# Block-diagonal local probabilities and strip-wise pooled scores in a fused attention and channel-mix kernel

## The chip, the cores and the metric

The kernel runs as one launch on one core of one Trainium2 chip. The metric is the device time of that core in microseconds: 724.21 as the median of three runs, from 723.01 to 724.3.

The engines are named as in the profile: PE is TensorE (PEld its weight loads), DVE is VectorE, ACT is ScalarE, POOL is GpSimd, SP is SyncE, which here only starts DMA transfers.

## What is computed

The reference, cut to what matters. q, k and v are (8, 8, 576, 64): batch, heads, positions, head size. The width of the second half is 512, its hidden width 1024.

```python
# attention, for each batch and head
q_d, k_d, v_d = means over groups of 4 positions       # 144 positions
out_up    = repeat(softmax(q_d @ k_d.T / 8) @ v_d, 4)  # pooled attention
scores    = where(abs(i - j) < 4, q @ k.T / 8, -1e9)   # local band
out_local = softmax(scores) @ v
x = (out_up + out_local), heads side by side           # (8, 576, 512)

# channel mix
x_prev = x shifted by one position, 0 at the start of each batch
xk = mu_k * x + (1 - mu_k) * x_prev
xr = mu_r * x + (1 - mu_r) * x_prev
k  = maximum(xk @ w_k, 0)
out = sigmoid(xr @ w_r) * ((k * k) @ w_v)
```

The weights `w_k`, `w_v`, `w_r` come as float64 and are turned into float32 on the chip.

## The kernel before, in words

**Pairs and chunks.** Attention goes by pairs of heads: pair n = 4b + p holds heads 2p and 2p + 1 of batch b, 32 pairs in all. The two heads of a pair are the two halves of the 128 partitions (64 values each) and are called e = 0, 1 in the code. The channel mix goes by 18 chunks of 256 rows (`CT`); a chunk starts when the pairs of its batch are done. In full stage the attention of later batches runs in between the chunks.

**A pair's steps.** SP loads q and k (`load_raw`, L279, a tile called raw with four buffers), v summed up as four planes (`load_v4`) and v in windows of 32 keys (`load_windows`, `vw`: 24 query positions need 30 keys; one window for each of the 24 groups of 24 queries of a head, four of them, i = 0 to 3, above each other on 4 x 32 partitions, six such columns g a head). DVE transposes q and k by blocks of 32 (`turn_q` L320, `turn_k` L325; two alternating tiles, `qT` and `kz`, by the parity of the pair; from pair 8 on, `SPLIT`, `kz` has two planes, one for each head with zeros in the other half, so that one product serves both heads). POOL pools q, k and v (`pool_q`, `pool_k`, `pool_v`; `pool_v` is on DVE for the first `VDVE` pairs). ACT copies the last 16 pooled queries of each head into a part of `qd` that is zero elsewhere (`last_q`, L351, two instructions at L356).

**Scores and softmax.** Pooled scores need 144 x 144 for each head. They lie in one PSUM bank as three column groups: `down_pe` (L465, products L468) makes the first 128 queries of each head with four products on quarters of the array (64 values deep, 64 queries wide); `down_last` (L457, product L461) makes the last 16 queries of both heads in one product over the whole array, 128 x 128, in which all but 32 of the 128 columns are zero. Local scores (`score_pe`, L389) are 24 products of 32 queries by 64 columns on four strips of 32 columns of the array (L400; before pair 8 one product for each head). Both softmaxes are worked out on DVE, ACT and POOL (`score_top` to `score_norm`, `down_top` to `down_norm`). Local probabilities are transposed on DVE (`score_turn`, tile `at`); `spread` (L451) copies them with four ACT instructions into `bd`, whose zeros are set once: there, two groups of 32 partitions each (i = 0, 1 and i = 2, 3) share 48 columns block by block. Pooled probabilities are transposed on PE (`down_turn`) and copied by ACT (`down_copy`, tile `adT`).

**Output of a pair.** `av_pe` (L519) makes the upsampled part, four products of 144 columns (L527, 72 positions deep, two accumulated for each head, on the two column halves of the array), and the local part, 24 products of 48 columns (L533), each 64 deep on one quarter of the array: r = 0, 1 for the halves of the partitions, e for the head. ACT copies the pooled part out of PSUM (`av_up`, L555, instruction L558), and DVE adds both into x (`av_out`, L560, two instructions at L566).

**The run.** In full stage PE takes the products of one pair and the output of the pair before it together: `run_pe` (L545) issues `down_last(n)`, `av_pe(n - 1)`, `down_pe(n)`, `score_pe(n)`. The first four pairs have `score_both` (L540) and `av_pe` apart; pair 4 begins with `score_both` alone.

**The channel mix.** `diff` (L583, on POOL for the first two chunks) subtracts neighbouring positions; ACT and DVE scale and add (`mix_part`, `mix_add`, `mix_high`, `mix_low`). Every float32 product of the mix is made as three products of a rounded type (F32R) of high parts and remainders: `k_pe` (L624, products L629), `r_pe` (L660), `v_pe` (L678). Remainders of the hidden values are `k_low` (L644, instruction L648), on DVE, or on POOL for the first chunk and for f in `KLF`. The weights are turned, rounded and split in the first 130 us (`weight_scale` to `weight_low`, L206 to L274): 20 tiles, `WORDER`; their remainders are made on PE and ACT (tiles in `LOWPE`), on DVE (`LOWDVE`) or on POOL.

**What sets the order.** `Plan` is a list scheduler that runs while the program is written. Each step is added with its engine, an assumed time, a rank (a wished time), the tiles that it reads and writes, and the buffers that it takes. `order()` takes the engine that can start first, and on it the ready step with the lowest rank. The resulting order is fixed: each engine works through its queue in that order and waits where a step's inputs are not there. `PER` is the wished time of a chunk, `STEP0` and `STEP1` the wished distances of the first pairs.

## Time and profile before

| | before |
|---|---|
| median of three runs | 724.21 us (723.01 to 724.3) |
| the profiled execution | 722.32 us |
| its span in the trace | 720.5 us |
| mean granted clock of TensorE | 0.959 |
| busy share PE / PEld | 92% / 78% |
| busy share DVE / ACT / POOL | 67% / 65% / 42% |
| bytes moved by DMA | 62.19 MB, mean 86 GB/s |

The page of the profile cuts the span in 40 slices of 18 us and gives the busy share of each engine in tenths (9 is 90% or more). A group of instructions is shown with its line, engine, output and inputs, its shape, how often it occurs, its busy time, the mean of one in ns, and the idle time of its engine just before, with what ended most of it. A row of the timeline has the start in us, a duration, engine, line and operation; a float32 product counts as two PE instructions. Matmuls are pipelined, so the starts of PE rows say more than their durations.

### The profile page before, as it was taken

How to read it: one execution, taken by the hardware profiler on the slowest of the kernel's cores; microseconds unless marked ns; L12 is line 12 of the kernel's file. 1: busy time of each engine (PE TensorE's matmuls, PEld its weight loads, DVE VectorE, ACT ScalarE, POOL GpSimd, SP SyncE). 2: the span in 40 equal slices, each digit the busy share in tenths (PEclk: the TensorE clock that was granted, in tenths of full speed). 3: DMA queues.
4: the chain of work that ended last, by engine and by line, in shares of the span. 5: the costliest groups of instructions: out<-in, count | busy, mean ns of one | idle time of the engine just before them, and what ended most of it. 6: DMA issues, size and time to landing. Idle time of an engine off the chain costs nothing.

```text
span 720.5 us, 18491 instructions
## 1 busy us (share of the span) xinstructions
PE 660.0 (92%) x7352; PEld 564.5 (78%) x7352; DVE 482.8 (67%) x863; ACT 465.0 (65%) x1159; POOL 299.4 (42%) x362
## 2 busy tenths in 40 slices
PE   2676785798999999999999999999999999999997
PEld 1543674686888888888888888888888888988986
DVE  3785899857975797579655688667866874464111
ACT  2464684677776877586567667586768676644442
POOL 5414398864454544454333266353565341000000
PEclk9977886799999999999999999999999999999999
DMA  8999944664435343433234163342451100000000
GB/s 138 175 245 186 217 126 105 114 117 79 103 63 114 77 95 70 110 67 82 60 70 96 40 134 73 93 81 77 80 120 40 53 2 31 1 30 30 0 30 30
DMA packets 221849, 62.19 MB, mean 86 GB/s; under 512 B 205123, under 2 KB 214595, under 8 KB 221763
## 3 DMA queue, kind: packets, MB, share of 16 engines
q1 hardware_dynamic: 221762, 61.01, 39.8%
q8 instruction: 58, 0.95, 0.6%
q14 instruction: 29, 0.23, 0.1%
HBM read 51.55 MB, written 9.44 MB: 85 GB/s over the span
## 4 chain that ended last, share of the span: by engine, by line
PE 76%; DVE 7%; ACT 4%; POOL 4%; DMA 3%; SPq 3%; issue 1%; POOLq 0%; ACTq 0%; DVEq 0%
PE ps_g L629 25%; PE acc L678 23%; PE ps_r L660 14%; PE ps_v L533 3%; PE ps_a L400 3%; PE ps_v L527 3%; SPq L286 2%; PE ps_a L461 1%; DMA v<-in_v_dram 1%; DMA stgx<-in_moe_w_k_dram 1%; ACT ad L485 1%; PE ps_a L468 1%; ACT L485 1%; PE ps_t L508 1%; DVE mxd L475 1%
## 5 line engine op out<-in xcount | busy, mean ns | idle before, releaser
L629 PE MATMUL ps_g<-xkh,wkh 128*128 128x256 f32 x576 | 165.6, 287 | 1.8 <-ACT xkh L616 1.5
L629 PE MATMUL ps_g<-xkl,wkh 128*128 128x256 f32 x576 | 162.5, 282 | 0.7 <-DVE xkl L621 0.7
L629 PE MATMUL ps_g<-xkh,wkl 128*128 128x256 f32 x576 | 162.0, 281 | 0.0
L648 DVE TENSOR_TENSOR kl<-kk,kh 128x256 fp32r<-128x256 f32 x119 | 65.9, 554 | 95.8 <-ACT kh L641 90.0
L678 PE MATMUL acc<-wvh,kh 128*128 128x512 f32 x288 | 115.9, 402 | 2.9 <-ACT kh L641 2.9
L678 PE MATMUL acc<-wvl,kh 128*128 128x512 f32 x288 | 114.6, 398 | 2.7 <-POOL wvl L274 2.7
L678 PE MATMUL acc<-wvh,kl 128*128 128x512 f32 x288 | 114.9, 399 | 2.1 <-DVE kl L648 1.2
L629 PEld LDWEIGHTS ps_g<-xkh,wkh 128*128 128x128 f32 x576 | 109.9, 191 | 7.8 <-ACT xkh L616 1.8
L629 PEld LDWEIGHTS ps_g<-xkl,wkh 128*128 128x128 f32 x576 | 109.8, 191 | 4.6 <-DVE xkl L621 1.0
L629 PEld LDWEIGHTS ps_g<-xkh,wkl 128*128 128x128 f32 x576 | 111.1, 193 | 0.0
L634 ACT ACTIVATE kk<-ps_g 128x256 f32<-128x256 f32 x144 | 55.0, 383 | 81.6 <-PE ps_g L629 78.8
L428 POOL TENSOR_TENSOR sm<-sm,mx 128x384 f32<-128x384 f32 x28 | 28.2, 1007 | 98.5 <-DVE mx L423 81.6
L648 POOL TENSOR_TENSOR kl<-kk,kh 128x256 fp32r<-128x256 f32 x25 | 21.2, 850 | 110.8 <-PE acc L678 81.3
L678 PEld LDWEIGHTS acc<-wvh,kl 128*128 128x128 f32 x288 | 54.9, 191 | 15.6 <-DVE kl L648 1.8
L678 PEld LDWEIGHTS acc<-wvh,kh 128*128 128x128 f32 x288 | 54.8, 190 | 12.5 <-ACT kh L641 3.3
L678 PEld LDWEIGHTS acc<-wvl,kh 128*128 128x128 f32 x288 | 54.9, 190 | 11.7 <-POOL wvl L274 3.1
L641 ACT ACTIVATE kh<-kk 128x256 fp32r<-128x256 f32 x144 | 60.2, 418 | 4.6
L640 ACT ACTIVATE kk<-kk 128x256 f32<-128x256 f32 x144 | 60.2, 418 | 4.3
L455 ACT ACTIVATE bd<-at 32x288 f32<-32x288 f32 x128 | 56.3, 440 | 9.6 <-DVE at L448 7.8
L475 DVE TENSOR_REDUCE mxd<-ps_a 128x3 f32<-128x432 f32 x32 | 19.4, 606 | 61.9 <-PE ps_a L400 56.9
L660 PE MATMUL ps_r<-wrh,xrh 128*128 128x512 f32 x144 | 57.6, 400 | 0.9 <-DVE sig L682 0.9
L660 PE MATMUL ps_r<-wrh,xrl 128*128 128x512 f32 x144 | 57.0, 396 | 0.0
(107 smaller groups left out, 1413.4 us busy)
## 6 DMA issues: line engine op xcount, KB each, us to landing
vw<-in_v_dram SPq DMA_DIRECT2D x126, 96.0 KB
qraw<-in_q_dram SPq DMA_DIRECT2D x128, 72.0 KB
kraw<-in_k_dram SPq DMA_DIRECT2D x128, 72.0 KB
v<-in_v_dram SPq DMA_DIRECT2D x32, 288.0 KB
out_dram<-sig SPq DMA_DIRECT2D x36, 256.0 KB
stg<-in_moe_w_k_dram SPq DMA_DIRECT2D x6, 512.0 KB
stgx<-in_moe_w_v_dram SPq DMA_DIRECT2D x4, 512.0 KB
stg<-in_moe_w_v_dram SPq DMA_DIRECT2D x4, 512.0 KB
```

The costliest lines, as they stand in the source:

```text
L400: nc.tensor.matmul(ps[32 * i:32 * i + 32, o:o + 64], qT[:, QT * j:QT * j + 32], kz[:, :, QT * j:QT * j + 32], start=True, stop=True)
L428: nc.gpsimd.tensor_tensor(out=s3, in0=s3, in1=mx[:, :, None].broadcast_to([P, 12, 32]), op=ALU.subtract)
L455: nc.scalar.activation(dst, src, AF.Copy)
L475: nc.vector.tensor_reduce(out=mx, in_=down_part(d["ps"]), axis=AX.X, op=ALU.max)
L527: nc.tensor.matmul(pv[0][64 * e:64 * e + 64, 288:432], d["vd"][:, 2 * e + kt, :], d["adT"][:, kt, 144 * e:144 * e + 144], start=(kt == 0), ...
L629: nc.tensor.matmul(ps, w[:, p, P * f:P * f + P], y[:, p, :], start=(m == 0), stop=(m == len(mm) - 1))
L634: nc.scalar.activation(kk, kq[c, f], AF.Relu)
L640: nc.scalar.activation(kk, kk, AF.Square)
L641: nc.scalar.activation(kh, kk, AF.Copy)
L648: eng.tensor_tensor(out=kl, in0=kk, in1=kh.bitcast(F32), op=ALU.subtract)
L660: nc.tensor.matmul(ps, y[:, p, P * t:P * t + P], w[:, p, :], start=(m == 0), stop=(m == len(mm) - 1))
L678: nc.tensor.matmul(accs[c][t], x[:, P * t:P * t + P], w[:, f, :], start=(f == 0 and m == 0), stop=(f == NF - 1 and m == 2))
```

## The change

Seven edits, made together:

1. **The local part of the output.** `bd` becomes 96 columns wide instead of 48, and `spread` puts each of the four groups of 32 partitions into 24 columns of its own, so that the whole 128 partitions form one block-diagonal matrix. `av_pe` takes 12 products of 96 columns, 128 deep, on the two column halves of the array (e), instead of 24 of 48 columns on quarters. The positions then lie in order in PSUM, and `av_out` reads and writes them in one stretch for each half.
2. **The pooled scores.** Pooled k is written into two planes (`kds`, one for each head, zeros in the other half), as `kz` is. `down_pe` makes the first 128 queries of each head with eight products of 32 queries on four strips of 32 columns of the array, and the last 16 queries with four more on the same strips. The product over the whole array (`down_last`) is gone, and with it `last_q` on ACT: `qd` is 176 columns wide, and the columns behind 144 are zeros, which the last strip reads along with the last 16 queries.
3. **The run.** `run_pe` issues `av_pe(n - 1)`, `down_pe(n)`, `score_pe(n)`; nothing of pair n stands ahead of the output of n - 1 any more, and pooled scores stand ahead of the local ones in `score_both` too.
4. **Buffers.** Raw q and k have three buffers instead of four.
5. **The band mask** is loaded twice by DMA into its double tile, instead of once and copied on POOL.
6. **Who makes what.** `LOWPE` takes weight tiles 9 and 11 as well, `LOWDVE` 8, 10, 12 and 14 (before, POOL made these six); `VDVE` is 2 instead of 4, so `pool_v` of pairs 2 and 3 goes to POOL; `KLF` is empty, so the `k_low` of f = 3 go to DVE.
7. **The planner's numbers**: `PER` 31.5 instead of 33.5, `STEP0` 6.0 and `STEP1` 0.0 instead of 4.0 and 4.0, and assumed times of the changed steps.

The diff, cut to its core:

```diff
-LOWPE = tuple(range(8))
-VDVE = 4
+LOWPE = (0,1,2,3,4,5,6,7,9,11)
+VDVE = 2
-LOWDVE = ()
+LOWDVE = (8,10,12,14)
-KLPOOL, KLF = 1, (3,)
+KLPOOL, KLF = 1, ()
-PER = 33.5
-STEP0, STEP1, W0, WSTEP = 4.0, 4.0, -25.0, 2.0
+PER = 31.5
+STEP0, STEP1, W0, WSTEP = 6.0, 0.0, -25.0, 2.0
...
-    qds = [cp.tile([P, 272], F32, name=f"qd{i}") for i in range(2)]
-    bd = cp.tile([P, 12, 48], F32, name="bd")
+    qds = [cp.tile([P, 176], F32, name=f"qd{i}") for i in range(2)]
+    kds = [cp.tile([P, 2, 144], F32, name=f"kd{i}") for i in range(2)]
+    bd = cp.tile([P, 12, 96], F32, name="bd")
...
-        raw = wp.tile([P, 18, 32], F32, tag="raw", name=nm + "raw", bufs=4)
+        raw = wp.tile([P, 18, 32], F32, tag="raw", name=nm + "raw", bufs=3)
...
-    def last_q(n):
-
-        qd = qds[n % 2]
-        for e in range(2):
-            h = slice(64 * e, 64 * e + 64)
-            nc.scalar.activation(qd[h, 144 + 16 * e:160 + 16 * e], qd[h, 128:144], AF.Copy)
-
...
-        nc.gpsimd.tensor_tensor(out=kd, in0=tk[:, :, 0], in1=tk[:, :, 1], op=ALU.add)
-        d["kd"] = kd
+        for e in range(2):
+            h = slice(64 * e, 64 * e + 64)
+            nc.gpsimd.tensor_tensor(out=kd[h, e, :], in0=tk[h, :, 0], in1=tk[h, :, 1], op=ALU.add)
...
-            dst, src = bd[32 * i:32 * i + 32, :, QT * (i % 2):QT * (i % 2) + QT], d["at"][32 * i:32 * i + 32, :, 0:QT]
+            dst, src = bd[32 * i:32 * i + 32, :, QT * i:QT * i + QT], d["at"][32 * i:32 * i + 32, :, 0:QT]
...
-        nc.tensor.matmul(ps[:, D0 + DP:D0 + DP + 144], d["qd"][:, 144:272], d["kd"], start=True, stop=True)
...
     def down_pe(n):
...
+        for t in range(4):
+            for e in range(2):
+                o = D0 + 2 * DP * e
+                nc.tensor.matmul(ps[32 * t:32 * t + 32, o:o + 144], qd[:, 32 * t:32 * t + 32], kd[:, e, :],
+                                 start=True, stop=True)
         for e in range(2):
-            for h in range(2):
-                o = D0 + 2 * DP * e
-                nc.tensor.matmul(d["ps"][64 * h:64 * h + 64, o:o + 144],
-                                 d["qd"][64 * e:64 * e + 64, 64 * h:64 * h + 64], d["kd"][64 * e:64 * e + 64, :],
-                                 start=True, stop=True)
+            o = D0 + DP
+            nc.tensor.matmul(ps[32 * e:32 * e + 32, o:o + 144], qd[:, 128:160], kd[:, e, :], start=True, stop=True)
+            nc.tensor.matmul(ps[64 + 32 * e:96 + 32 * e, o:o + 144], qd[:, 144:176], kd[:, e, :], start=True, stop=True)
...
         for g in range(NG):
-            for r in range(2):
-                h = slice(64 * r, 64 * r + 64)
-                for e in range(2):
-                    nc.tensor.matmul(pv[r][64 * e:64 * e + 64, 48 * g:48 * g + 48],
-                                     d["vw"][h, 6 * e + g, :], bd[h, 2 * g + e, :], start=True, stop=True)
+            for e in range(2):
+                nc.tensor.matmul(pv[g // 3][64 * e:64 * e + 64, 96 * (g % 3):96 * (g % 3) + 96],
+                                 d["vw"][:, 6 * e + g, :], bd[:, 2 * g + e, :], start=True, stop=True)
...
     def run_pe(n):
-        down_last(n)
-        av_pe(n - 1)
-        down_pe(n)
-        score_pe(n)
+        av_pe(n - 1)
+        score_both(n)
```

How instructions move. The queue of PE in a run of full stage, between two groups of products of the mix, before the change: `kd` and `qd` are pooled k and q, `adT` and `bd` the probabilities, `vd` and `vw` the values.

```order
L461 MATMUL ps_a<-kd,qd_76 128x144
L527 MATMUL ps_v<-adT,vd 64x144 x4
L533 MATMUL ps_v<-bd,vw 64x48 x24
L468 MATMUL ps_a<-kd,qd_76 64x144 x4
L400 MATMUL ps_a<-kz_79,qT_82 32x64 x24
```

The same run after the change:

```order
L518 MATMUL ps_v<-adT,vd 64x144 x4
L522 MATMUL ps_v<-bd,vw 64x96 x12
L457 MATMUL ps_a<-kd_77,qd_75 32x144 x8
L461 MATMUL ps_a<-kd_77,qd_75 32x144
L462 MATMUL ps_a<-kd_77,qd_75 32x144
L461 MATMUL ps_a<-kd_77,qd_75 32x144
L462 MATMUL ps_a<-kd_77,qd_75 32x144
L393 MATMUL ps_a<-kz_80,qT_83 32x64 x24
```

The product over the whole array at the head is gone, the local part has half as many products of twice the columns, and the pooled scores are twelve products in a row.

The queue of ACT at the end of the first batch, before the change. The last `av_up` of the batch (L558, second row of that line) stands behind `last_q` of pair 4 (L356); L241, L259 and L269 turn weights.

```order
L558 ACTIVATE up<-ps_v 128x144
L269 ACTIVATE wkl<-ps_w 128x512
L259 ACTIVATE wkh<-w_612 128x512
L259 ACTIVATE wkh<-w_753 128x512
L241 ACTIVATE w_793<-stgx 128x512
L269 ACTIVATE wkl<-ps_w 128x512
L241 ACTIVATE w_838<-stgx 128x512
L356 ACTIVATE qd_75<-qd_75 64x16 x2
L558 ACTIVATE up<-ps_v 128x144
L259 ACTIVATE wvh<-w_793 128x512
```

The same place after the change, with `av_up` at L545:

```order
L545 ACTIVATE up<-ps_v 128x144
L448 ACTIVATE bd<-at 32x12x24 x4
L509 ACTIVATE adT<-ps_t 72x288 x2
L266 ACTIVATE wkl<-ps_w 128x512
L256 ACTIVATE wkh<-w_642 128x512
L238 ACTIVATE w_771<-stg 128x512
L545 ACTIVATE up<-ps_v 128x144
L256 ACTIVATE wkh<-w_692 128x512
L266 ACTIVATE wkl<-ps_w 128x512
```

Between the last two `av_up` of the batch, `last_q` is gone and fewer weight steps stand there.

The queue of POOL at the same place, before the change; L587 is `diff` of the first chunk, L373 and L374 are `pool_v`, L348 to L365 pool q and k of pair 4.

```order
L373 TENSOR_TENSOR v_657<-v_657 72x4x128
L374 TENSOR_TENSOR vd<-v_657 72x256
L348 TENSOR_TENSOR tq<-qT_81 128x288
L349 TENSOR_TENSOR qd_75<-tq 128x144
L364 TENSOR_TENSOR tk<-kz_78 128x288
L365 TENSOR_TENSOR kd<-tk 128x144
L373 TENSOR_TENSOR v_717<-v_717 72x4x128
L374 TENSOR_TENSOR vd<-v_717 72x256
L587 TENSOR_TENSOR dx<-xt 128x1024
L648 TENSOR_TENSOR kl<-kk,kh 128x256
```

The same place after the change, with `diff` at L573 and `pool_v` at L365 and L366:

```order
L365 TENSOR_TENSOR v_660<-v_660 72x4x128
L366 TENSOR_TENSOR vd<-v_660 72x256
L573 TENSOR_TENSOR dx<-xt 128x1024
L365 TENSOR_TENSOR v_714<-v_714 72x4x128
L366 TENSOR_TENSOR vd<-v_714 72x256
L634 TENSOR_TENSOR kl<-kk,kh 128x256
```

`diff` stands ahead of the second `pool_v` instead of behind it, and pooling of q and k of pair 4, ahead of `diff` before, comes behind these rows.

More of the change, by code (lines that the diff above doesn't have):

```diff
@@ L394, in score_pe @@
             for e in range(2):
-                nc.tensor.matmul(ps[:, S1 * e:S1 * e + 32 * NG], idn, mask, start=True, stop=False)
+                nc.tensor.matmul(ps[:, S1 * e:S1 * e + 32 * NG], idn, mask2[:, :, 0, :], start=True, stop=False)
         for j in range(4 * NG):
@@ L510, in down_turn @@
             nc.tensor.matmul(ps.rearrange("p (e c) -> p e c", e=2)[:, :, 128:144], ak[1],
-                             idn[:, 0:32].rearrange("p (e c) -> p e c", e=2), start=True, stop=True)
+                             idn[:, 0:64].rearrange("p (e c) -> p e c", e=2)[:, :, 0:16], start=True, stop=True)
     def down_copy(n):
@@ L529, in av_pe @@
         for g in range(NG):
-            for r in range(2):
-                h = slice(64 * r, 64 * r + 64)
-                for e in range(2):
-                    nc.tensor.matmul(pv[r][64 * e:64 * e + 64, 48 * g:48 * g + 48],
-                                     d["vw"][h, 6 * e + g, :], bd[h, 2 * g + e, :], start=True, stop=True)
+            for e in range(2):
+                nc.tensor.matmul(pv[g // 3][64 * e:64 * e + 64, 96 * (g % 3):96 * (g % 3) + 96],
+                                 d["vw"][:, 6 * e + g, :], bd[:, 2 * g + e, :], start=True, stop=True)
         d["pv"] = pv
@@ L540, in score_both, with run_pe @@
     def score_both(n):
-        down_last(n)
-        score_pe(n)
-        down_pe(n)
-    def run_pe(n):
-        down_last(n)
-        av_pe(n - 1)
+        st[n]["ps"] = pp.tile([P, 1024], F32, tag="att", name="ps_a", bufs=1)
         down_pe(n)
         score_pe(n)
+    def run_pe(n):
+        av_pe(n - 1)
+        score_both(n)
     def new_x(b):
@@ L686, in store_out @@
         nc.sync.dma_start(outf[r0:r0 + P, :], gates[c][t])
-    plan = Plan(dict(raw=4, v4=2, vw=3, kd=2, sm=2, ad=1, adT=1, at=1, up=2, vd=2, xt=2, f32tmp=2, xkh=2,
+    plan = Plan(dict(raw=3, v4=2, vw=3, sm=2, ad=1, adT=1, at=1, up=2, vd=2, xt=2, f32tmp=2, xkh=2,
                      xkl=2, xrh=1, xrl=1, kk=2, kh=4, kl=4, sig=3, g=2, acc0=1, acc1=1, c0=1, c1=1, att=1))
@@ L722, in pair_scores @@
             add("POOL", 1.2, R - 7, pool_q, n, r=[f"qT{i}"], w=[f"qd.{i}"])
-            add("ACT", 0.42, R - 6, last_q, n, w=[f"qd.{i}"])
-            add("POOL", 1.4 if n < SPLIT else 2.0, R - 6, pool_k, n, r=[f"kT{i}"], new=[(f"kd{n}", "kd")])
+            add("POOL", 1.9 if n < SPLIT else 2.4, R - 6, pool_k, n, r=[f"kT{i}"], w=[f"kd.{i}"])
             add(*(("DVE", 1.0) if n < VDVE else ("POOL", 2.15)), R1 - 8, pool_v, n, r=[f"v4{n}"], new=[(f"vd{n}", "vd")])
@@ L851, in begin_all @@
     def begin_all():
-        add("SP", 1.0, -110, load_consts, w=["mask", "idn"])
-        add("POOL", 2.2, -110, clear, w=["kT0", "kT1", "qT0", "qT1", "qd.0", "qd.1", "bd"])
+        add("SP", 1.5, -110, load_consts, w=["mask", "idn"])
+        add("POOL", 2.2, -110, clear, w=["kT0", "kT1", "qT0", "qT1", "qd.0", "qd.1", "kd.0", "kd.1", "bd"])
         add("SP", 1.0, W0, load_mus, w=["mu"])
@@ L857, in attention_moe @@
     add("ACT", 0.3, -60, turn_sign, r=["idn"], w=["nidn"])
-    add("POOL", 1.0, -60, double_mask, r=["mask"], w=["mask2"])
     for i in range(len(WORDER)):
@@ L879, in attention_moe @@
                 else:
-                    add("PE", 3.3 if n < SPLIT else 2.85, at_run[n], run_pe, n, **join(av_of(n - 1), s))
+                    add("PE", (3.0 if n < SPLIT else 2.6) - 0.15, at_run[n], run_pe, n, **join(av_of(n - 1), s))
                     pair_scores(n - 1, 2)
```

24 lines of the change are left out of this document (9 added, 15 removed).

## The prediction

> **What bounds the kernel now.** I read the page first (busy shares, slices, the chain that ended last), then the windows, then single stretches of the timeline. On the page:
>
> ```profile
> PE 660.0 (92%) x7352; PEld 564.5 (78%) x7352; DVE 482.8 (67%) x863; ACT 465.0 (65%) x1159; POOL 299.4 (42%) x362
> ...
> PE   2676785798999999999999999999999999999997
> ...
> PE 76%; DVE 7%; ACT 4%; POOL 4%; DMA 3%; SPq 3%; issue 1%; POOLq 0%; ACTq 0%; DVEq 0%
> ```
>
> TensorE carries three quarters of the chain, and its holes lie in the first eight of 40 slices. The windows put numbers to that; the columns are the busy times of PE, PEld, DVE, ACT and POOL, then clock, DMA share and GB/s:
>
> ```profile
> 60.00:80.00 20.00, 12.17 (x134) 8.06 (x135) 13.72 (x18) 13.48 (x28) 6.29 (x8) 0.67 1.00 187
> 80.00:100.00 20.00, 16.22 (x80) 13.34 (x79) 17.49 (x21) 13.39 (x34) 14.67 (x11) 0.81 0.72 189
> 100.00:120.00 20.00, 15.90 (x222) 12.39 (x220) 19.17 (x26) 13.89 (x36) 18.45 (x18) 0.83 0.54 131
> 120.00:135.00 15.00, 6.58 (x171) 5.27 (x171) 13.84 (x20) 7.94 (x19) 12.82 (x15) 0.56 0.49 88
> 135.00:180.00 45.00, 42.17 (x489) 35.69 (x490) 30.30 (x60) 33.60 (x85) 26.74 (x35) 0.99 0.53 103
> 180.00:600.00 420.00, 417.37 (x4807) 363.44 (x4806) 304.73 (x560) 297.44 (x750) 192.43 (x232) 1.00 0.35 77
> ```
>
> So there are two stages with different limits. From 135 on TensorE is idle for 2.8 us of 45 and 2.6 us of 420: there every microsecond that its instructions gain or lose is a microsecond of the end, and DVE, ACT and POOL have a quarter or more of their time free. Before 135 TensorE waits; DMA is full to 80, DVE and POOL are nearly full from 80 to 135. There only an earlier arrival of 134.9 counts, where the second chunk's first product (L629) starts and TensorE stays busy. The forecast is the sum of the two.
>
> **Part 1: the run of small products after 135.** A run (`run_pe`) in the full stage, block by block; the column behind the start is the modelled busy time, so I take starts:
>
> ```profile
> 324.14 0.41 PE L461 MATMUL ps_a<-kd,qd 128*128 128x144 f32 x2
> 324.48 0.71 PE L527 MATMUL ps_v<-adT,vd 72*64 72x144 f32 x8
> 325.12 0.91 PE L533 MATMUL ps_v<-bd,vw 64*64 64x48 f32 x48
> 325.86 0.44 PE L468 MATMUL ps_a<-kd,qd 64*64 64x144 f32 x8
> 326.23 0.88 PE L400 MATMUL ps_a<-kz,qT 128*32 128x64 f32 x48
> 327.04 0.39 PE L629 MATMUL ps_g<-xkh,wkh 128*128 128x256 f32 x1
> ```
>
> The blocks take 0.34, 0.64, 0.74, 0.37 and 0.81, together 2.90 us. A float32 product is two passes, so the count is double. How long a pass is, the last two rounds of L527 show (two narrow windows):
>
> ```profile
> 324.78 0.41 PE L527 MATMUL ps_v<-adT,vd 72*64 72x144 f32 x4
> ```
>
> ```profile
> 324.90 0.29 PE L527 MATMUL ps_v<-adT,vd 72*64 72x144 f32 x2
> ```
>
> A round (one pass on each column half at the same time) of 144 columns takes 0.12 us, 0.85 ns a column. L461 is two passes one behind the other, 0.24, in 0.34: a block that ends with another split of the array costs about 0.10 more. L468 is two rounds on four quarters, 0.24, in 0.37: 0.10 for its end and 0.03 for the first round after a switch.
>
> The new run, term by term: the switch from the big products to column halves, 0.10 (now paid behind L461); the upsampled part, unchanged, 0.64 less its closing switch, 0.54, as the local part now uses the same halves; the local part, 12 products = 24 passes of 96 columns on two halves = 12 rounds of 0.08, with its switch 1.08 (0.74 now); the pooled scores, 12 products = 24 passes on four strips = 6 rounds of 0.12 and 0.03, 0.75 (0.34 + 0.37 = 0.71 now); the local scores, 0.81 less the 0.02 to 0.03 of a first round, 0.79, as they already run on strips. Sum 3.26: **0.36 us more a run**. Four quarters at work become two halves, with twice the columns, and that costs more than the switch saved. From below: L533's rounds take 0.74/12 = 0.06 where 48 columns would need 0.04, so something besides columns limits them; were 96 columns to cost no more rounds than that, the local part would be 0.84 and the pooled scores 0.71, and the run 2.98, still 0.08 up. From above see the second rival. Pairs 7 to 31 have 25 runs after 135: 25 x 0.36 = 9.0, and the last local part by itself 0.2: **+9.2 us** (2 at the least).
>
> Hidden in this stage, by the free time of the window 180 to 600 (DVE 115 us, ACT 123, POOL 228):
>
> ```profile
> L356 ACT ACTIVATE qd<-qd 64x16 f32<-64x16 f32 x64 | 13.5, 211 | 24.7 <-POOL qd L349 24.2
> L365 POOL TENSOR_TENSOR kd<-tk 128x144 f32<-128x144 f32 x32 | 17.7, 555 | 2.5
> L648 DVE TENSOR_TENSOR kl<-kk,kh 128x256 fp32r<-128x256 f32 x119 | 65.9, 554 | 95.8 <-ACT kh L641 90.0
> ```
>
> ACT loses the 64 copies of `last_q` (13.5 us); POOL writes pooled k in two halves, at most 32 more additions of 0.56 (18 us); DVE takes the 17 `k_low` of f = 3 from POOL (9.4 us). `spread` writes as many elements, `av_out` as many. All nothing here, and a few tenths each if DVE's cover went. Three raw buffers: SP's queue waits for the transpose of the third load back; 25 runs in the 465 us from 135 to 600 are one in 18 us or so, and DMA is a third full, so nothing; otherwise a late `turn_k` would stop TensorE at the next run, in front of the pooled scores.
>
> **Part 2: the start.** Where the time to 134.9 is lost now: the last attention output of the first batch.
>
> ```profile
> 55.38 0.71 PE L527 MATMUL ps_v<-adT,vd 72*64 72x144 f32 x8
> 56.02 0.92 PE L533 MATMUL ps_v<-bd,vw 64*64 64x48 f32 x48
> ```
>
> ```profile
> 61.47 0.44 ACT L356 ACTIVATE qd<-qd 64x16 f32<-64x16 f32 x2 [4.41 <-POOL qd L349]
> 61.93 0.29 ACT L558 ACTIVATE up<-ps_v 128x144 f32<-128x144 f32 x1
> ```
>
> ```profile
> 62.26 0.82 DVE L566 TENSOR_TENSOR xt<-ps_v,up 128x288 f32<-128x288 f32 x2 [4.14 <-ACT up L558]
> ```
>
> ```profile
> 58.25 1.26 POOL L373 TENSOR_TENSOR v<-v 72x512 f32<-72x512 f32 x1 [11.28 <-DMA v<-in_v_dram]
> 59.59 0.72 POOL L374 TENSOR_TENSOR vd<-v 72x256 f32<-72x256 f32 x1
> ...
> 66.59 1.26 POOL L373 TENSOR_TENSOR v<-v 72x512 f32<-72x512 f32 x1 [3.90 <-DMA v<-in_v_dram]
> 67.93 0.72 POOL L374 TENSOR_TENSOR vd<-v 72x256 f32<-72x256 f32 x1
> 68.62 1.89 POOL L587 TENSOR_TENSOR dx<-xt 128x1024 f32<-128x1024 f32 x1
> ```
>
> The product is done at 56.9, but `av_up` stands in ACT's queue behind `last_q` of the next pair, which waits for POOL and that for a load; and on POOL `diff` stands behind a second `pool_v`, which waits for its load until 66.6. With `last_q` gone, x could be whole at 56.9 + 0.29 + 0.82 = 58.0. In the new POOL order `diff` stands behind one `pool_v` only, that of pair 4, done at 60.3. So `diff` starts at 60.3, not 68.6: **8.3 us earlier**, bound by the same load as now. The two chances that x is later than 60.3 (two `pool_v` moved from DVE to POOL, 2.0 us each, ahead of the norms of pairs 2 and 3; two more words to write per pooled k, 4 x 0.56) have 2.3 us of slack.
>
> How much of that reaches 134.9? From 80 on POOL and DVE hold it:
>
> ```profile
> 128.50 1.29 POOL L365 TENSOR_TENSOR kd<-tk 128x144 f32<-128x144 f32 x1
> ```
>
> ```profile
> 134.90 0.58 PE L629 MATMUL ps_g<-xkh,wkh 128*128 128x256 f32 x1
> ```
>
> ```profile
> L274 POOL TENSOR_TENSOR wvl<-w,wvh 128x512 fp32r<-128x512 f32 x4 | 6.9, 1722 | 1.2 <-PE ps_g L629 1.2
> L274 POOL TENSOR_TENSOR wkl<-w,wkh 128x512 fp32r<-128x512 f32 x4 | 6.6, 1642 | 4.0 <-ACT wkh L259 4.0
> L682 DVE TENSOR_TENSOR sig<-acc,sig 128x512 f32<-128x512 f32 x36 | 23.9, 682 | 5.0 <-PE acc L678 4.9
> ```
>
> POOL is rid of six weight remainders (four k, two v: 4 x 1.64 + 2 x 1.72 = 10.0 us), DVE gets four of them, by its nearest row of this width 0.68 each, 2.7 us, and TensorE two, in its idle time. DVE is the fuller engine (19.17 of 20), so its 2.7 count. But DVE's steps are longer beside POOL's:
>
> ```profile
> 108.53 1.64 DVE L255 SCALAR_TENSOR_TENSOR w<-stgx,w 128x512 int32<-128x512 int32 x1
> ```
>
> ```profile
> 115.12 0.69 DVE L255 SCALAR_TENSOR_TENSOR w<-stg,w 128x512 int32<-128x512 int32 x1
> ```
>
> The first ran while POOL was busy, the second in POOL's pause: up to 0.95 apiece, 5.7 for the six. I take a quarter, 1.4, since POOL has other work to put there. So the start gains 8.3 - 2.7 + 1.4 = **7.0 us**. From below 0 (if all of it is lost again by 134.9), from above about 13: 8.3 and half of POOL's 10.0.
>
> **Sum.** +9.2 - 7.0 = +2.2. The profiled execution took 722.32 us for a span of 720.5; the median of the runs is 724.21, 1.9 above it. So 724.5 for such an execution, and 726.4 as a median.
>
> **Rivals.**
>
> *POOL's relief decides (faster).* The last wait before 134.9 is for POOL (pooled k, 128.50 to 129.79, behind those eight remainders and more). If POOL and not DVE is what limits 100 to 135, the start gains 13 and not 7: 9.2 - 13 = -3.8, 720.4. For it: 18.45 of 20 on POOL. Against: DVE's 19.17. It decides from a gain of 9.2 on; the second chunk's first product would start before 125.7.
>
> *The strips go one after another (much slower).* The new loop issues both heads' products of a strip, four passes, before the next strip. If a strip holds one waiting pass beside the running one and the third stops the queue, each strip starts 0.24 behind the one before and the block ends after 1.44, not 0.75: 0.69 x 25 = 17 more, 743.6. For it: no row has four passes in a row on one part of the array with others behind. Against: L468's passes come in pairs on each quarter and still ran four at a time: 0.37; in strict order of program they would take 4 x 0.12 + 0.12 = 0.60. The Trainium skill, "TensorE: Matmul & The Clock Gate", Part 3 (packing small matmuls), says that matmuls start and end in program order without reordering; the trace of L468 does not agree. By that rule the block would take 2.04, the run 1.3 more, 32 in all, 758.7 us; after L468's row I give it 0.02 of the 0.21 below.
>
> *The start gives nothing.* With three raw buffers the k load of pair 5 waits for the transpose of pair 4's q, which in the new DVE order stands behind the first chunk's mixing; if pairs 5 and 6 then arrive as late as now or nearly, a start gain of 0 to 2 leaves +9.2 to +7.2: 732. For it: DMA is full until 80. Against: pair 5's run stands behind the first chunk's k products and most of its v products in both orders.
>
> **Chances and range.** Forecast 0.42, faster rival 0.27, strips 0.21, start 0.10. A measurement of this kernel tells 0.2%, 1.4 us, from no change. The forecast's own spread (about 3 us: the quarter taken of 5.7, the 0.08 to 0.36 of the run) gives 0.29 slower, 0.11 same, 0.02 faster; the faster rival 0.26 faster and 0.01 same; the strips 0.21 slower; the last 0.07 slower and 0.03 same. Together 0.28 faster, 0.15 same, 0.57 slower. The range goes from 717 (the faster rival with a start gain of 16, 8.3 and most of POOL's 10.0) to 745 (the strips at their price); the forecast's own is 722 to 731.
>
> **What would show it.** In the changed profile: the local part's 24 passes take about 1.0 us from their first start to that of the pooled scores, in a full run; the pooled scores 0.75 (1.4 or 2.0: the strips); the whole run 3.26. `diff` of the first chunk starts near 60.3, and the second chunk's first `ps_g` product near 128; after it TensorE is idle for no more than some 6 us to the end. I am wrong if the run is not longer than 2.98, if that product starts before 125.7 or after 132, or if a wait for q or k raw data shows in front of a run.

## The result, and the profile after

The changed kernel takes 732.52 us as the median of four runs (731.45 to 733.98), beside 723.61 (720.89 to 724.3) for the kernel before. The ratio is 1.0126, with an interval from 1.0107 to 1.0145: slower by 1.3%, or 9 us. The profiled execution after took 732.89 us with a span of 731.1; before it was 722.32 and 720.5, so between the two traces there are 10.6 us.

The forecast was 726.4 and the range 717 to 745: the sign and the range held, and the size did not; the forecast's own spread, 722 to 731, was missed from above. Of its two parts the run came out at its forecast price of 0.36 us within a few hundredths, and the start with the wrong sign. The boundary is the second chunk's first product, which before started at 134.90. These are the rows of the two traces that fix the parts; first the changed kernel's timeline of TensorE, a wait and that product:

```profile
134.06 1.23 PE L518 MATMUL ps_v<-adT,vd 72*64 72x144 f32 x8 [11.31 <-DVE xt L551]
...
139.70 0.39 PE L615 MATMUL ps_g<-xkh,wkh 128*128 128x256 f32 x1
```

So the start lost 4.8 us (139.70 against 134.90) where 7.0 were to be gained. From there to the end it is 731.1 - 139.70 = 591.4 us, against 720.5 - 134.90 = 585.6 before: 5.8 more, where 9.2 were forecast.

**The run.** A run in the full stage of the changed kernel, block by block (start, modelled busy time):

```profile
307.52 0.28 PE L615 MATMUL ps_g<-xkh,wkl 128*128 128x256 f32 x1
307.73 0.71 PE L518 MATMUL ps_v<-adT,vd 72*64 72x144 f32 x8
308.27 1.16 PE L522 MATMUL ps_v<-bd,vw 128*64 128x96 f32 x24
309.36 0.72 PE L457 MATMUL ps_a<-kd,qd 128*32 128x144 f32 x16
309.87 0.30 PE L461 MATMUL ps_a<-kd,qd 128*32 128x144 f32 x2
...
310.12 0.87 PE L393 MATMUL ps_a<-kz,qT 128*32 128x64 f32 x48
310.92 0.39 PE L615 MATMUL ps_g<-xkh,wkh 128*128 128x256 f32 x1
```

From start to start: upsampled part 0.54, local part 1.09, pooled scores 0.76, local scores 0.80. The last product of the mix ahead of it is followed after 0.21 instead of the usual 0.12, which is the switch of some 0.10. Together 3.29 us, against 2.90 before.

**Waits of TensorE after 135**, grouped by who releases them; before the change:

```profile
PE ps_t L508 <- POOL ad L496: 3.1, 4, 1.1
PE acc L678 <- DVE kl L648: 1.2, 1, 1.2
PE ps_r L660 <- DVE sig L682: 0.9, 2, 0.6
PE ps_g L629 <- ACT kk L634: 0.3, 1, 0.3
```

and after it:

```profile
PE ps_t L500 <- POOL ad L488: 1.1, 1, 1.1
PE ps_r L646 <- DVE sig L668: 0.7, 2, 0.5
```

5.5 us have become 1.8. That is 3.7 us which the forecast did not have, and it offset part of the run's price: 25 x 0.39 = 9.75, less 3.7, is 6.1, close to the 5.8 measured.

**The start.** In the changed kernel POOL's `diff` (L573), behind the `pool_v` of pair 4:

```profile
62.71 1.26 POOL L365 TENSOR_TENSOR v<-v 72x512 f32<-72x512 f32 x1 [11.96 <-DMA v<-in_v_dram]
64.05 0.72 POOL L366 TENSOR_TENSOR vd<-v 72x256 f32<-72x256 f32 x1
64.73 1.89 POOL L573 TENSOR_TENSOR dx<-xt 128x1024 f32<-128x1024 f32 x1
```

and what waits for it on DVE, the first `mix_add`, while the steps on weights stand behind it:

```profile
68.39 1.23 DVE L598 TENSOR_TENSOR xk<-xk,xt 128x1024 f32<-128x1024 f32 x1 [7.87 <-ACT xk L584]
69.53 1.77 DVE L247 SCALAR_TENSOR_TENSOR w<-stgx,w 128x512 int32<-128x512 int32 x1
```

`diff` starts at 64.7, where the forecast had 60.3 and the kernel before 68.6. DVE, the engine with the most work in this stage, stands still for 7.9 us. The whole account of DVE up to the second chunk's first product (window; busy time of PE, PEld, DVE, ACT, POOL; clock, DMA share, GB/s) is, before the change

```profile
0.00:134.90 134.90, 83.62 (x1311) 62.19 (x1311) 103.21 (x162) 75.90 (x193) 74.64 (x89) 0.79 0.83 166
```

and after it

```profile
0.00:139.70 139.70, 83.93 (x1270) 62.61 (x1271) 100.89 (x162) 73.64 (x179) 76.03 (x95) 0.80 0.80 159
```

DVE has 162 instructions in both. Its busy time went down from 103.2 to 100.9 us and its idle time up from 31.7 to 38.8. Busy and idle time add up to the window by definition, so the account says where the loss lies, idle time, and not yet why. Two entries of the list of idle times in these windows, by line, show the largest part of it (x count, busy time, mean ns, and the idle time just before); before the change

```profile
L323 DVE STREAM_TRANSPOSE qT<-qraw 128x576 f32<-128x576 f32 x8 | 6.1, 760 | 7.1 <-DMA qraw<-in_q_dram 7.1
L612 DVE TENSOR_TENSOR xk<-xk,xt 128x1024 f32<-128x1024 f32 x2 | 2.4, 1208 | 1.5 <-ACT xk L598 1.5
```

and after it

```profile
L320 DVE STREAM_TRANSPOSE qT<-qraw 128x576 f32<-128x576 f32 x8 | 6.1, 764 | 10.6 <-DMA qraw<-in_q_dram 10.6
L598 DVE TENSOR_TENSOR xk<-xk,xt 128x1024 f32<-128x1024 f32 x2 | 3.5, 1754 | 7.9 <-ACT xk L584 7.9
```

The hole in front of the mix grew by 6.4 us. Waits of DVE for the loads of q, k and v grew from 11.1 to 18.7 in all, and its waits for ACT's `av_up` shrank from 5.0 to 0.8.

### The profile page after: what moved, and what is told of

Its sections match the earlier page's. It is cut to its first block, busy times and chain, and to the rows that moved or that the text cites. A ratio compares the mean times of both kernels' runs of the same rounds, so it can differ in the third digit from the quotient of the medians.

```text
span 731.1 us, 17865 instructions
## 1 busy us (share of the span) xinstructions
PE 669.8 (92%) x7038; PEld 582.2 (80%) x7038; DVE 482.7 (66%) x880; ACT 452.3 (62%) x1097; POOL 298.1 (41%) x375
## 4 chain that ended last, share of the span: by engine, by line
PE 81%; DVE 6%; issue 4%; DMA 3%; ACT 2%; SPq 2%; POOL 2%; DVEq 0%; ACTq 0%; POOLq 0%
PE ps_g L615 27%; PE acc L664 24%; PE ps_r L646 14%; PE ps_v L522 4%; PE ps_a L457 3%; PE ps_v L518 3%; PE ps_a L393 2%; SPq L283 1%; DMA stgx<-in_moe_w_k_dram 1%; ACT ad L477 1%; DVE w L247 1%; PE ps_t L500 1%; PE ps_a L461 1%; DMA kraw<-in_k_dram 1%; PE ps_t L501 1%
## 5 line engine op out<-in xcount | busy, mean ns | idle before, releaser
L634 DVE TENSOR_TENSOR kl<-kk,kh 128x256 fp32r<-128x256 f32 x136 | 71.8, 530 | 103.9 <-ACT kh L627 103.2
L664 PE MATMUL acc<-wvh,kl 128*128 128x512 f32 x288 | 113.3, 393 | 2.8 <-POOL kl L634 2.7
L664 PE MATMUL acc<-wvl,kh 128*128 128x512 f32 x288 | 112.4, 390 | 1.1 <-POOL wvl L271 1.1
L615 PEld LDWEIGHTS ps_g<-xkh,wkl 128*128 128x128 f32 x576 | 108.8, 189 | 0.0
L477 ACT ACTIVATE ad<-ps_a,mxd 128x144 f32<-128x144 f32 x96 | 35.4, 377 | 44.3 <-DVE sm L411 21.8
```

What stands on the lines that cost most here:

```text
L477: nc.scalar.activation(ad[:, t, :], ps[:, t, :], AF.Exp, scale=1.0 / 128, bias=mx[:, t:t + 1], accum_out=sd[:, t:t + 1])
L615: nc.tensor.matmul(ps, w[:, p, P * f:P * f + P], y[:, p, :], start=(m == 0), stop=(m == len(mm) - 1))
L634: eng.tensor_tensor(out=kl, in0=kk, in1=kh.bitcast(F32), op=ALU.subtract)
L664: nc.tensor.matmul(accs[c][t], x[:, P * t:P * t + P], w[:, f, :], start=(f == 0 and m == 0), stop=(f == NF - 1 and m == 2))
```

## The experiments

Three theories stood at the beginning. One: the new order and sharing out of work (the planner's numbers) lose the start. Two: the new structure loses it, three raw buffers above all. Three: the hole of 7.9 us in DVE's queue is the loss. In the run the question was how the 0.39 us divide between the two edits. Ratios are to the kernel before, on the same chip and in the same rounds; a difference of ratios is given in us as its share of 723.6.

**1. The numbers alone** (kernel before):

```diff
-LOWPE = tuple(range(8))
-VDVE = 4
-LOWDVE = ()
-KLPOOL, KLF = 1, (3,)
-PER = 33.5
-STEP0, STEP1, W0, WSTEP = 4.0, 4.0, -25.0, 2.0
+LOWPE = (0,1,2,3,4,5,6,7,9,11)
+VDVE = 2
+LOWDVE = (8,10,12,14)
+KLPOOL, KLF = 1, ()
+PER = 31.5
+STEP0, STEP1, W0, WSTEP = 6.0, 0.0, -25.0, 2.0
```

> The kernel before with the new planner's numbers and sharing out alone (PER, STEP0, STEP1, LOWPE, LOWDVE, VDVE, KLF); products, last_q, four raw buffers as before. The run of small products should stay 2.90 us. Theory A (the start is lost by the new order, whatever the structure: a hole in DVE's queue in front of the first chunk's mix and four weight remainders more on DVE): the second chunk's first product comes at 138 to 140, as in the changed kernel (139.7), and the holes of TensorE after it are small (about 2 us as in the changed kernel, 5.5 before), so about 723.6 + 4.8 - 3.6 = 724.8. Theory B (the start is lost by the structure, the three raw buffers above all): the second chunk's first product comes at 128 to 130, as forecast, and the time is about 723.6 - 6 - 3.6 = 714.

718.82 us, ratio 0.9919 (0.9893 to 0.9945): faster by 5.9 us, between the two expectations. The trace of TensorE:

```profile
128.44 1.23 PE L527 MATMUL ps_v<-adT,vd 72*64 72x144 f32 x8 [2.88 <-DVE xt L566]
...
132.72 0.58 PE L629 MATMUL ps_g<-xkh,wkh 128*128 128x256 f32 x1
```

The start gains 2.2 us and the rest 2.1 (716.2 - 132.72 = 583.5). The first theory falls: the numbers are the good part of the change. `diff` starts at 60.7 here:

```profile
60.66 1.89 POOL L587 TENSOR_TENSOR dx<-xt 128x1024 f32<-128x1024 f32 x1
```

That is the forecast's 60.3, with `last_q` still in place: the new order of POOL and ACT brings it, not the missing `last_q`.

**2. The structure alone** (changed kernel, the same six lines put back):

> The changed kernel with the planner's numbers and sharing out of before; its products, two-plane pooled k, no last_q, three raw buffers. The run should be 3.29 us as in the changed kernel, 9.8 us more over the whole. Theory A (the new numbers lose the start): the second chunk's first product at 133 to 135, the holes of TensorE after it as before, so about 723.6 + 9.8 = 733. Theory B (the structure loses it): at 139 to 140, so about 723.6 + 9.8 + 4.8 = 738.

736.63 us, ratio 1.0162 (1.0136 to 1.0189), with the second chunk's first product at 141.07. That is near the second theory's time and place: the structure costs at the start too. In this trace DVE stands idle for 11.6 us in front of the first `mix_add`, which starts at 75.13.

**3. Local part back on quarters** (changed kernel):

```diff
-    bd = cp.tile([P, 12, 96], F32, name="bd")
+    bd = cp.tile([P, 12, 48], F32, name="bd")
...
-            for e in range(2):
-                nc.tensor.matmul(pv[g // 3][64 * e:64 * e + 64, 96 * (g % 3):96 * (g % 3) + 96],
-                                 d["vw"][:, 6 * e + g, :], bd[:, 2 * g + e, :], start=True, stop=True)
+            for r in range(2):
+                h = slice(64 * r, 64 * r + 64)
+                for e in range(2):
+                    nc.tensor.matmul(pv[r][64 * e:64 * e + 64, 48 * g:48 * g + 48],
+                                     d["vw"][h, 6 * e + g, :], bd[h, 2 * g + e, :], start=True, stop=True)
```

(`spread` and `av_out` as before, too.)

> The changed kernel with its local part alone put back: 24 products of 48 columns on quarters of the array, bd 48 columns wide, the order of all instructions else as in the changed kernel. Theory A (blocks add up): the run is 0.10 + 0.64 + 0.74 + 0.76 + 0.80 = 3.04 us instead of 3.29, so 0.25 x 25 + 0.25 = 6.5 us less than the changed kernel, 726. Theory B (the switch from quarters to strips costs more than the one from halves, or the local part hides some of what stands behind it): the run is 3.15 or more and the time 729 or more. The second chunk's first product stays at 139 to 140 either way.

726.93 us, ratio 1.0035 (1.0021 to 1.0049). The run in its trace:

```profile
305.44 0.71 PE L518 MATMUL ps_v<-adT,vd 72*64 72x144 f32 x8
306.08 0.91 PE L524 MATMUL ps_v<-bd,vw 64*64 64x48 f32 x48
306.93 0.72 PE L457 MATMUL ps_a<-kd,qd 128*32 128x144 f32 x16
...
307.69 0.87 PE L393 MATMUL ps_a<-kz,qT 128*32 128x64 f32 x48
308.49 0.39 PE L618 MATMUL ps_g<-xkh,wkh 128*128 128x256 f32 x1
```

0.10 + 0.64 + 0.85 + 0.76 + 0.80 is 3.15, as the second theory had it. The same 24 products of the local part took 0.74 before, where a block on quarters (L468) followed, and take 0.85 here, where strips follow. So the local part costs 0.15 a run and the pooled scores 0.24 (means of the 25 runs of each trace), and not 0.25 and 0.15 as adding up single blocks had it. After the second chunk's first product, at 138.42, there are 726.3 - 138.42 = 587.9 us: 3.5 less than in the changed kernel, and 25 x 0.15 is 3.75. The time is all the same that of the first theory, 726: the ratios differ by 6.6 us, so some 3 us more were gained ahead of that product, where the plan is the same; no run shows why.

**4. `diff` ahead of `pool_v`** (changed kernel, POOL's order alone):

```diff
     emitted = plan.order()
+    late = emitted.pop(at("pool_v", NP))
+    emitted.insert(at("diff", 0) + 1, late)
```

> The changed kernel with one step moved: on POOL, diff of the first chunk stands ahead of pool_v of pair 4 instead of behind it, so it no longer waits for that v load. Theory A (the hole in DVE's queue from 60.5 to 68.4, in which the mix waits for diff, is what the start lost): diff starts at 57 to 58 instead of 64.8, the hole shrinks from 7.9 to 1 or 2 us, the second chunk's first product comes at 133 to 134 instead of 139.7, and the time is 726 to 727. Theory B (DVE and the loads have their pace whatever stands there; the hole only moves): the first chunk's first product comes earlier, the second chunk's stays at 138 to 140, and the time stays within 2 us of 732.5.

727.59 us, ratio 1.0046 (1.0030 to 1.0062): 5.8 us less than the changed kernel. `diff` on POOL, and the mix on DVE:

```profile
55.41 1.89 POOL L573 TENSOR_TENSOR dx<-xt 128x1024 f32<-128x1024 f32 x1 [6.26 <-DVE xt L551]
```

```profile
60.87 2.10 DVE L598 TENSOR_TENSOR xk<-xk,xt 128x1024 f32<-128x1024 f32 x1 [0.17 <-ACT xk L584]
```

The hole has gone from 7.87 to 0.17. The account of DVE up to the second chunk's first product:

```profile
0.00:135.27 135.27, 83.79 (x1271) 63.04 (x1271) 105.58 (x162) 73.73 (x179) 75.49 (x94) 0.85 0.79 163
```

Idle time fell by 9.1 us, from 38.8 to 29.7, and the same 162 instructions took 4.7 us longer; the product came 4.4 earlier. The third theory holds for this kernel, at about half of the hole: what DVE no longer waits it partly loses in steps that last longer.

**5 and 6. Raw buffers**: four instead of three in the kernel of experiment 3, and three instead of four in that of experiment 1, each in the planner's count of buffers as well.

```diff
-        raw = wp.tile([P, 18, 32], F32, tag="raw", name=nm + "raw", bufs=3)
+        raw = wp.tile([P, 18, 32], F32, tag="raw", name=nm + "raw", bufs=4)
```

> The changed kernel with its local part put back to quarters, as in the run of that name before, and raw with four buffers instead of three; nothing else. That run had its second chunk's first product at 138.4, 726.9 us. Theory A (three raw buffers delay the loads behind them on SP, and so the v load for which diff waits; DVE then idles): with four the second chunk's first product comes at 132 to 134 and the time is about 721. Theory B (the loads are late for another reason, the band mask loaded twice ahead of all or the load of the DMA queues itself): it stays at 137 to 138.5 and the time at 726 to 727.

> The kernel before with the new planner's numbers (718.8 us, second chunk's first product at 132.7, idle time of DVE up to there 30 us) and raw with three buffers instead of four; nothing else. Theory A (three raw buffers lose the start): the second chunk's first product comes at 137 to 139, with DVE idle for 35 us or more up to there, and the time is about 724. Theory B (they do not): 132 to 133.5, time 718 to 720.

With four, 727.64 us, ratio 1.0067 (1.0047 to 1.0086), against 1.0035 with three. With three, 718.89 us, ratio 0.9938 (0.9918 to 0.9958), against 0.9919 with four. Neither gains from the fourth buffer by more than the intervals. The profiled execution of the second, the longest of its five runs, has the second chunk's first product at 136.18 against 132.72, while the medians differ by 0.1 us: a place in the start, read from one execution, is good to two or three us only. In both pairs of traces three buffers go with a later load: the v load of pair 4 is issued at 57.92 instead of 54.04 in the kernel of experiment 1, with DVE idle for 37.1 us instead of 30.5, and at 57.11 instead of 54.94 in that of experiment 3. So a price of three raw buffers is not shown by the times, and one of two us or so is not excluded.

**7. `diff` ahead of `pool_v` in the kernel of experiment 1** (the same two lines as in 4):

> The kernel before with the new planner's numbers, and diff of the first chunk ahead of pool_v of pair 4 on POOL; nothing else. Theory A (an earlier diff is worth what it takes from DVE's idle time, here the hole of 1.5 us in front of the first mix): diff at 55 to 57 instead of 60.7, the second chunk's first product at 131 to 132 instead of 132.7, the time 717 to 718. Theory B (an earlier diff by itself carries through): the second chunk's first product 4 to 5 us earlier, at 128, and 714.

719.74 us, ratio 0.9952 (0.9935 to 0.9969): no gain, though `diff` starts at 55.1. The second chunk's first product is at 135.09, so neither expectation came. Where there was no long hole in front of the mix (1.5 us), an earlier `diff` bought nothing. From that product to the end it is 583.5 us here, 583.6 in experiment 6 and 583.5 in experiment 1: the 3.6 us between these three executions lie in the start.

**8. The band mask loaded once** (changed kernel):

```diff
-        for e in range(2):
-            nc.sync.dma_start(mask2[:, :, e, :], band)
+        nc.sync.dma_start(mask2[:, :, 0, :], band)
...
+        nc.gpsimd.tensor_copy(out=mask2[:, :, 1, :], in_=mask2[:, :, 0, :])
```

> The changed kernel with the band mask loaded once by DMA and copied on POOL, as before the change (one copy instead of two); nothing else. The first q load is issued at 2.81 in the changed kernel and at 1.66 before. Theory A (the second mask load moves all loads by its 1.15 us and no more): the second chunk's first product at 138.5 instead of 139.7, the time 731 to 732. Theory B (the head's delay grows in the full DMA queues to the 3 to 4 us by which the loads are late at 34 us): 136, and 729. Theory C (it is absorbed, since the loads wait for raw buffers anyway): 139.7, 732.5.

730.87 us, ratio 1.0116 (1.0095 to 1.0137), 0.7 us better by the ratios and 1.6 by the medians, within the intervals. In its trace the v load of pair 4 is issued at 55.36 instead of 57.99 and the second chunk's first product is at 137.58, but by the time none of the three expectations is excluded.

**9. What is left are the pooled scores** (changed kernel with the local part, the raw buffers and the mask put back as in 3, 5 and 8):

> The changed kernel with three parts put back: local part on quarters, four raw buffers, the band mask loaded once. Against the kernel before with the new planner's numbers (718.8 us, second chunk's first product at 132.7, run 2.90) what is left of the change is the pooled scores on strips: pooled k in two planes, the twelve products, no last_q, the new order in the run. Theory A (the parts add up): the run is 3.14 us, 0.24 x 25 = 6 us more; the mask's 2 us go from the 137.4 of the kernel with two masks, so the second chunk's first product is at 135.4 and the time 726: pooled scores cost 2 to 3 us at the start as well, by longer scores of the first pairs. Theory B (the start is lost by the mask and the raw buffers alone): 132.7 as in the kernel with the numbers alone, and 723.5.

726.96 us, ratio 1.0031 (1.0012 to 1.0051), the time of the first expectation; its place, 135.4, was missed by 2.9 us (138.33). Against experiment 1 the pooled scores differ, with what belongs to them (pooled k in two planes, no `last_q`, the order of the run, and the order of the queues that follows), and the ratio goes from 0.9919 to 1.0031: 8.1 us. The account of DVE in experiment 1 and here:

```profile
0.00:132.72 132.72, 81.61 (x1316) 59.60 (x1316) 102.21 (x162) 76.39 (x193) 69.36 (x86) 0.83 0.87 168
```

```profile
0.00:138.33 138.33, 84.90 (x1415) 61.72 (x1415) 101.39 (x162) 73.49 (x179) 75.26 (x95) 0.81 0.78 161
```

Same instructions, 0.8 us less busy time, 6.4 us more idle time (30.5 to 36.9). After that product 587.9 us remain instead of 583.5: 6.0 of the run, less the waits that went (3.7 to 1.8). The 5.6 us ahead of it are too many: the trace here is of the longest of seven executions, that of experiment 1 of a short one, and the 8.1 of the ratios less these 4.4 leave 3.7 for the start. The hole in front of the mix is 6.9 us here and 1.5 in experiment 1, although the mix starts only 1.5 us later (65.82, 64.32). Part of the difference is one of booking: in experiment 1 the step ahead of it is drawn out beside `diff` on POOL (60.66 to 62.55), and the row counts as busy time.

```profile
60.04 2.80 DVE L246 TENSOR_SCALAR w<-w 128x512 int32<-128x512 int32 x1
```

Without POOL beside it the same step takes 0.42 us.

**10. Four remainders from DVE to TensorE and ACT** (kernel of experiment 1):

```diff
-LOWPE = (0,1,2,3,4,5,6,7,9,11)
-LOWDVE = (8,10,12,14)
+LOWPE = (0,1,2,3,4,5,6,7,8,9,10,11,12,14)
+LOWDVE = ()
```

> The kernel before with the new planner's numbers, and the four weight remainders that those put on DVE (8, 10, 12, 14) made on TensorE and ACT instead. Theory A (DVE paces the start: the second chunk's first product comes when DVE's busy and idle time up to there have passed): DVE is rid of 4.9 us, the second chunk's first product comes at 128 to 129 instead of 132.7, and the time is about 714.5. Theory B (DVE only fills its time; loads and weight buffers pace it, or ACT does, which gets four copies of 0.64): 132 to 133.5, and 718 to 720, with DVE's idle time longer by what it was relieved of.

713.78 us, ratio 0.9870 (0.9853 to 0.9887): the best of all kernels here, 3.5 us better than experiment 1 by the ratios (5.0 by the medians) and 9.4 better than the kernel before.

```profile
0.00:129.74 129.74, 86.36 (x1328) 62.66 (x1328) 98.29 (x158) 78.08 (x199) 70.74 (x86) 0.81 0.87 172
```

DVE has 3.9 us less to do, idles 31.4 instead of 30.5, and the product comes 3.0 earlier. This is the first expectation: less work on DVE brings the start's end nearer here, though the order of the queues was planned anew with it.

**11. All remainders of w_k and w_v on TensorE and ACT** (`LOWPE = tuple(range(16))`):

> The kernel before with the new planner's numbers and the remainders of all of w_k and w_v (weight tiles 0 to 15) on TensorE and ACT; POOL keeps the four of w_r, DVE none. Against the run with only 8, 10, 12 and 14 moved (713.8 us, second chunk's first product at 129.7), POOL is rid of two more, some 3 us. Theory A (DVE paces the start and POOL matters only by drawing out DVE's steps): a gain of 0 to 1 us, 713 to 714. Theory B (POOL is on the path near 130): 2 to 3 us earlier, 711. Against both: ACT, which gets two copies of 0.6 more, binds, and the time is above 715.

720.57 us, ratio 0.9959 (0.9940 to 0.9978), 6.4 us worse than the step before; of the expectations only the last has its time, and that ACT binds is not shown. The order turned out differently: TensorE took the second chunk's first products ahead of the run of pair 5 and waited for ACT there.

```profile
125.48 0.58 PE L629 MATMUL ps_g<-xkh,wkh 128*128 128x256 f32 x1 [3.95 <-ACT xkh L616]
...
129.25 0.68 PE L461 MATMUL ps_a<-kd,qd 128*128 128x144 f32 x2
```

More waits follow in the next chunks (5.6 us from 130 on). How much of the loss is ACT's work and how much the order was not separated.

**12. Experiment 10's edit in the changed kernel:**

> The changed kernel (732.5 us, second chunk's first product at 139.7) with the remainders of weight tiles 8, 10, 12 and 14 on TensorE and ACT instead of DVE; nothing else. Theory A (DVE paces the start here as well): DVE is rid of 4 us, the second chunk's first product comes 3 us earlier, at 136 to 137, and the time is 728 to 729.5. Theory B (here the hole in DVE's queue and the run at half clock set the end, not DVE's work): 139 to 140 and 731 to 733.

731.44 us, ratio 1.0099 (1.0075 to 1.0123), between the expectations.

```profile
136.30 0.38 PE L615 MATMUL ps_g<-xkh,wkh 128*128 128x256 f32 x1
```

The start gains 3.4 us, as DVE's relief would have it, but 730.1 - 136.30 = 593.8 us follow instead of 591.4: two thirds of the gain go again behind it, where TensorE waits for 4.0 us instead of 1.8.

## Why the prediction was right and where it was wrong

Put in a chain, experiment by experiment, the change divides so:

| step | ratio | us |
|---|---|---|
| the planner's numbers | 1 to 0.9919 | -5.9 |
| pooled scores on strips, order of the run | 0.9919 to 1.0031 | +8.1 |
| mask loaded twice | 1.0031 to 1.0067 | +2.6 |
| three raw buffers | 1.0067 to 1.0035 | -2.3 |
| local part block-diagonal | 1.0035 to 1.0126 | +6.6 |

The steps compare runs of different rounds, and each is uncertain by some 2 to 3 us, so the mask and the raw buffers are not told from nothing; the other three are. Of the 6.6 of the local part the run explains 3.75.

**Right: the run.** The forecast's terms were 0.10, 0.54, 1.08, 0.75 and 0.79, together 3.26; measured are 0.10, 0.54, 1.09, 0.76 and 0.80, together 3.29. The reason given (half of the array in two pieces with twice the columns costs more than the saved switch) is what the blocks show. Taken block by block its terms give the local part 0.24 and the pooled scores 0.14, and there it was wrong: 0.15 and 0.24. The closing switch of the quarters was booked with the pooled scores (the 0.10 in L468's 0.37), so it seemed to go with them; but the last block on quarters pays it, and with strips behind it the local part takes 0.85 instead of 0.74.

**Right: the strips run together.** The twelve products with 24 passes take 0.76, not 1.44 or more. The Trainium skill, "TensorE: Matmul & The Clock Gate", Part 3, has matmuls start and end strictly in program order; by the prediction's reading of that rule the block would have taken 2.04, and the trace does not agree.

**Missing: the waits in the full stage.** The forecast took the 5.4 us of idle time after 135 as given. They shrank by 3.7. From the second chunk's first product on they are 3.7 us with the numbers alone (experiment 1), 3.3 with the structure alone (experiment 2) and 1.8 with the numbers and the pooled scores (experiment 9): each brings about half, in one trace each.

**Wrong: the start.** The step that failed is "`diff` starts at 60.3, not 68.6: 8.3 us earlier, bound by the same load as now", and with it the start's gain of 7.0: the second chunk's first product came after 132, which the prediction itself had named as a sign of being wrong. x was whole at 57.1 (forecast 58.0), but the load did not come when it did before. SP's queue, changed kernel:

```profile
54.43 3.47 SPq L283 DMA_DIRECT2D kraw<-in_k_dram  x4
57.99 0.41 SPq L292 DMA_DIRECT2D v<-in_v_dram  x1
```

and before:

```profile
48.93 4.93 SPq L286 DMA_DIRECT2D kraw<-in_k_dram  x4
53.96 0.41 SPq L295 DMA_DIRECT2D v<-in_v_dram  x1
```

The v load of pair 4 is issued 4.0 us later, so `pool_v` starts at 62.7 instead of 58.3 and `diff` gains 3.9 us, not 8.3. The second mistake was larger: that a gain of `diff`, less DVE's new work, is a gain at 134.9. The first `mix_add` did start 3.9 us earlier, at 68.39 instead of 72.28. But DVE had been busy for 36.3 us by then instead of 45.2, and from there to the second chunk's first product it took 71.3 us instead of 62.6. The prediction looked for the bound of the start in the busy shares from 80 to 135 and did not ask what DVE would wait for ahead of them. Its terms for DVE's work were mis-sized as well, but not to its harm: the four remainders took 4.3 us and not 2.7, and the 60 steps on weights 48.1 instead of 52.0, 3.9 less, where 1.4 was taken; two `pool_v` left. Yet DVE idled 7.1 us more. Of that, experiment 4 shows the hole in front of the mix, worth 4.4 us of the start and 5.8 of the time.

A second loss stands at the end of the stage, and here the change adds a wait that was not named: `run_pe` now has all of its products behind the wait for the x of the pair before (11.31 us in the changed kernel), since `av_pe` comes first and needs the two banks. From there to the second chunk's first product it takes 139.70 - 134.06 = 5.64 us; in experiment 1, where L461 is done ahead of that wait, 132.72 - 128.44 = 4.28. In the kernel before, the last wait stood in front of L461 as well, and it took 134.90 - 129.84 = 5.06, so against it the loss is 0.6.

**The rivals.** POOL's relief did come (14.57 us busy from 100 to 120 instead of 18.45), and the second chunk came later all the same; that rival falls. Up to the second chunk's first product POOL was busy for 76.0 us instead of 74.6, since two `pool_v` and the second half of pooled k came to it. "The start gives nothing" had 732 us, which is the measured time, but by another mechanism: it wanted a gain of 0 to 2 at the start, undone by three raw buffers that hold back pairs 5 and 6, and experiments 5 and 6 show no price of three buffers in the times. Its time was met by luck: a loss of 4.8 at the start and 3.7 us of waits saved later came together. The wide range held by luck too, since its upper end, 745, was the price of the strips one after another, which did not happen.

**Open.** Why the second chunk's first product comes later with the pooled scores on strips (experiment 9; 5.6 us in the traces, 3.7 by the ratios) is shown only in part, and so is why the loads of the first pairs come later in the changed kernel. The run behind the wait is some 1.0 of it (138.33 - 133.07 = 5.26 us in experiment 9, 4.28 in experiment 1); the rest lies in small delays of the first pairs, their loads and the mix, which no run separated. Nor was it tried whether the changed kernel gains from taking a part of the pooled scores ahead of that wait.

## What to carry to other kernels

For a block of small products the price is passes times columns plus a switch wherever the split of the array changes, and it is counted over the whole sequence, since a switch belongs to two neighbours; done so, the sum came out to 0.03 us. For narrow blocks the price of a pass is read from a row: 48 columns on quarters took 0.06 us a round, not the 0.04 of their columns. For a start in which several engines are nearly full, keep an account of the one with the most work from time 0, busy and idle, and ask of every edit what that engine then waits for: here 3.9 us less work on DVE brought the end of the start 3.0 us nearer, and a hole of 7.9 us in front of one step, with other work behind it in the queue, cost 4.4.
